# Sum and difference of the token transform made in the filter's last step; the feature transform's product order and its neighbours rearranged

## The chip, the cores and the metric

One of the cores of a Trainium2 chip runs the whole program. The metric is the device time in microseconds (us), as the median of several executions. Matrix products run on PE (TensorE; its weight loads are shown as PEld), element-wise work on DVE (VectorE), ACT (ScalarE) and POOL (GpSimd). SP issues most of the transfers, ACT and POOL a few. Every engine takes its instructions in program order and waits for the others through semaphores.

## The reference

The input x has 2048 tokens of 576 features, in fp32. Four residual layers follow each other, A, B, A, B. A is a layer norm, a sliding-window attention with 32 heads and an output projection. B is a layer norm and a global filter: a 2D real Fourier transform over tokens and features, a product with complex weights, and the transform back. Cut to that:

```python
def _B_ref(x, w_r, w_i):
    X = jnp.fft.rfft2(x, axes=(-2, -1))
    X = X * (w_r + 1j * w_i)
    return jnp.fft.irfft2(X, (S, D), axes=(-2, -1))
x = x + _A_ref(_layernorm(x), A_wqkv, A_wo)
x = x + _B_ref(_layernorm(x), B_w_r, B_w_i)
x = x + _A_ref(_layernorm(x), A_wqkv, A_wo)
x = x + _B_ref(_layernorm(x), B_w_r, B_w_i)
```

## The kernel before, in words

The change lies in `layer_b`, which runs twice. All transforms are products with constant matrices on PE. Where full precision matters, a factor is split into a high part (rounded to 12 bits, type fp32r, by ACT) and a low part (the rest, by DVE), and the product is made as high x high, high x low and low x high.

The 2048 tokens are 16 tiles of 128, token = 16 p + n2 for tile n2. Three stages follow each other.

*Filter stage* (the feature transform and the first half of the token transform), tile by tile, with the attention layer's last projection (`out.unit`, tile `ops`) running ahead in the same loop. For a tile `f0` normalises (`xn`, ACT L198; the mean and deviation come from `out.sums` on DVE and a square root on ACT L622) and folds even and odd features (`eo`, POOL L200, L202). `f1` transposes (PE L214 to L216, tile `tp`) and splits (`et`: ACT L219 high, DVE L220 low, ACT L221 a tail of 33 features). `f2` makes the feature transform `pf` (PE L231, L232: seven products for each of two halves) and splits it (`yh` ACT L235, `yl` DVE L236). `f3` makes the first half of the token transform `pz` (PE L243, six products), takes `half` out of PSUM (ACT L246), makes the sum and difference of the two halves on DVE (L247, L248) and stores them to `yd` in DRAM. In a loop for t = 1 to 11, `f1`, `f2` and `f3` of tiles t, t and t - 1 stand between the steps of later tiles; the last tiles (12 to 15) have a loop of their own, the tail. The PSUM tile `tp` has one buffer, and the turn of the attention output (`out.ahead`, tile `tpo`) uses it too.

*Mixing stage* (the filter itself), in 16 groups of frequencies. `g1m` makes a product over 16 tokens (`p`, PE L325), multiplies it by the complex weights (DVE L331 to L333) and adds the parts to `uv` (POOL L335, L336). Two groups later `g2` transforms back (`pq`, PE L347), copies the result out (`ye`, ACT L350) and stores it to `yd[1]` (L362; from ACT's queue for groups 0 to 8 and the even ones after, from SP's for the rest). The order within a turn is `g2`, `g1m`, loads.

*Inverse stage*, again in 16 tiles. `ly` loads a tile; two turns later `i0` makes the sum and difference of its two halves (POOL L382, L383, tile `both`) and splits them (ACT L384, DVE L385, and small tails L386, L387) into one of three buffers `z`, a part of `oroom`. Two turns on `i1` makes the second half of the token transform `pi` (PE L398, 18 products) and splits it (`zh` ACT L404, L406, `zl` DVE L405, L407). One turn on `i2` makes the inverse feature transform `po` (PE L418, L422, 16 products), copies one half (`bs`, ACT L425), adds the residual (DVE L426, L427) and finishes the output tile `xo` (POOL L428, L429). Program order in a turn is `ly`, `i1`, `i2`, `i0`:

```python
pipe(NT, [(0, ly), (4, i1), (5, i2), (2, i0)], lambda t: t in OPEN and nxt and next(nxt))
```

In the first of the two passes the last argument puts the opening of the next attention layer (loads, and the statistics of its first tiles) into the later turns.

Of the kernel before, what the change touches and what calls it, by code (L numbers as in the profile page):

```python
# [8 lines left out]
F32 = mybir.dt.float32  # L9
# [7 lines left out]
DF = 289  # L17
NF = 290
# [106 lines left out]
def layer_b(tc, src, dst, dcs, gc, ident, rh, rl, out, ic_d, fc_d, ga_d, m2_d, w_d, dram, nxt, share):  # L125
# [3 lines left out]
    V, A, T, P = nc.vector, nc.scalar, nc.tensor, nc.gpsimd  # L129
# [4 lines left out]
    with ExitStack() as stack:  # L134
        banks, inner = ExitStack(), ExitStack()
        ip = stack.enter_context(tc.tile_pool(name="bi", bufs=1))
        cp = inner.enter_context(tc.tile_pool(name="bc", bufs=1))
        wp = inner.enter_context(tc.tile_pool(name="bw", bufs=2))
        pp = banks.enter_context(tc.tile_pool(name="bps", bufs=2, space=PSUM))
# [42 lines left out]
        def pre(n2):  # L182

            if n2 in (1, 4, 7, 10):
                k = (1, 4, 7, 10).index(n2)
                e = 4 * k + 4 + k // 3
                nc.sync.dma_start(fc[:, 4 * k:e].rearrange("p g j c m -> p (g j c m)"), fc_d[:, 1024 * k:256 * e])
            if n2 in (2, 6, 9, 12):
                k = (2, 6, 9, 12).index(n2)
                e = 4 * k + 4 + k // 3  # L190
                nc.sync.dma_start(m2[:, 4 * k:e].rearrange("p g c m -> p (g c m)"), m2_d[:, 1024 * k:256 * e])
            if n2 % 2 and n2 // 2 < NW:
                pre_w(n2 // 2)

        def f0(n2, h):
            x, r, n = out.stats(n2)
            xn = ip.tile([128, D], F32, tag="ta", name=f"xn{n2}", bufs=3)
            A.activation(xn, x, AF.Identity, bias=n, scale=r)  # L198
            eo = h["eo"] = eos[n2 % 4]
            P.tensor_add(eo[:, 0, 1:288], xn[:, 1:288], xn[:, 575:288:-1])  # L200
            A.copy(eo[:, 0, 0:289:288], xn[:, 0:289:288])
            (P if n2 else V).tensor_sub(eo[:, 1, 0:287], xn[:, 1:288], xn[:, 575:288:-1])  # L202

            tl = h["tl"] = ip.tile([128, 2, 3, 33], F32, tag="td", name=f"tl{n2}", bufs=4)
            e = eo[:, :, 256:289]
            P.tensor_copy(tl[:, :, 0].bitcast(F32R), e)
            P.tensor_copy(tl[:, :, 2].bitcast(F32R), e)
            P.tensor_sub(tl[:, :, 1].bitcast(F32R), e, tl[:, :, 0])
# [14 lines left out]
        def f2(n2, h):  # L223
            ps = pp.tile([128, 2, 512], F32, tag="mm", name=f"pf{n2}", bufs=3)
            et = h["et"]
            for c in range(2):
                o = ps[:, c, 0:NF]
                b = 5 * c
                seq = [(0, 0), (0, 2), (2, 0), (1, 1), (1, 3), (3, 1)]
                for q, (si, mi) in enumerate(seq):  # L230
                    T.matmul(o, et[:, c, si], dcs[(b + mi) // 2][:, (b + mi) % 2], start=q == 0, stop=False)  # L231
                T.matmul(o, et[0:99, c, 4], dcs[(b + 4) // 2][0:99, (b + 4) % 2], start=False, stop=True)  # L232
            h["yh"] = yh = ip.tile([128, 2, NF], F32R, tag="yh", name=f"yh{n2}", bufs=3)
            h["yl"] = yl = ip.tile([128, 2, NF], F32R, tag="yl", name=f"yl{n2}", bufs=3)
            A.copy(yh, ps[:, :, 0:NF])  # L235
            V.tensor_sub(yl, ps[:, :, 0:NF], yh.bitcast(F32))  # L236

        def f3(n2, h):
            pz = pp.tile([128, 2, 512], F32, tag="mm", name=f"pz{n2}", bufs=3)
            yh, yl = h["yh"], h["yl"]  # L240
            for j in (1, 0):
                for k, (t, y) in enumerate(((0, yh), (0, yl), (1, yh))):
                    T.matmul(pz[:, j, 0:NF], gc[:, t, j], y[:, j], start=k == 0, stop=k == 2)  # L243
            ye = wp.tile([128, 2, NF], F32, tag="ye", name=f"ye{n2}", bufs=3)
            half = ip.tile([128, 2, NF], F32, tag="both", name=f"half{n2}", bufs=2)[:, 0]
            A.copy(half, pz[:, 1, 0:NF])  # L246
            V.tensor_add(ye[:, 0], pz[:, 0, 0:NF], half)  # L247
            V.tensor_sub(ye[:, 1], pz[:, 0, 0:NF], half)  # L248
            yef = ye.rearrange("p j f -> p (j f)")
            pre(n2)  # L250
            if n2 == FD:
                nc.sync.dma_start(y_tile(0)[0:8 * FD].rearrange("p a c f -> p a (c f)"), yd[0][0:2, 0:FD].rearrange("a n i f -> (n i) a f"))
            if n2 >= FD:
                for g in range(2):
                    (nc.scalar if n2 == NT - 1 else nc.sync).dma_start(ys[g][8 * n2:8 * n2 + 8].rearrange("p c f -> p (c f)"), yef[8 * g:8 * g + 8])
            nc.sync.dma_start(yd[0][:, n2], yef)
# [8 lines left out]
        hs = [dict() for _ in range(NT)]  # L265
# [19 lines left out]
        for t in range(1, NT - 4):  # L285
            u = t + 4
            out.unit(u, pp)
            f1(t, hs[t])
            if t == 1:
                norm(4)  # L290
                f3(0, hs[0])
                out.ahead(6, pp)
            out.sums(u)
            if t > 1:
                f3(t - 1, hs[t - 1])
            f0(u, hs[u])
            f2(t, hs[t])
            out.ahead(u + 2, pp)
        f1(NT - 4, hs[NT - 4])
# [3 lines left out]
        nc.sync.dma_start(ic.rearrange("p a f -> p (a f)").bitcast(F32), ic_d.rearrange("p a f -> p (a f)").bitcast(F32))  # L303
        nc.sync.dma_start(ga.rearrange("p a j c -> p (a j c)").bitcast(F32), ga_d.bitcast(F32))
        for t in range(NT - 4, NT + 1):
            for v, f in ((t, f2), (t + 1, f1), (t - 1, f3)):
                if v < NT:
                    f(v, hs[v])
        warm(24)
# [10 lines left out]
        def g1m(g, h):  # L320
            ps = pp.tile([128, 2, 512], F32, tag="mm", name=f"p2_{g}", bufs=3)

            for c in range(2):
                for j in range(2):
                    T.matmul(ps[64 * j:64 * j + 64, c, 0:NF], fc[:, g, j, c], h["y"][:, j], start=True, stop=g > 0)  # L325
                    if g == 0:
                        T.matmul(ps[64 * j:64 * j + 64, c, 0:NF], fc[:, 16, j, c], h["y"][:, 1 - j], start=False, stop=True)
            w = wt[g]
            p1 = tws[g % 2]
            p2 = wp.tile([128, 2, NF], F32, tag="tc", name=f"p2_{g}", bufs=3)  # L330
            V.tensor_mul(p1, ps[:, :, 0:NF], w)  # L331
            V.tensor_mul(p2[:, 0], ps[:, 0, 0:NF], w[:, 1])
            V.tensor_mul(p2[:, 1], ps[:, 1, 0:NF], w[:, 0])  # L333
            h["uv"] = uv = ip.tile([128, 2, NF], F32, tag="ta", name=f"uv{g}", bufs=3)
            P.tensor_sub(uv[:, 0], p1[:, 0], p1[:, 1])  # L335
            P.tensor_add(uv[:, 1], p2[:, 0], p2[:, 1])  # L336
# [3 lines left out]
        def g2(g, h):  # L340
            pq = pp.tile([128, 2, 512], F32, tag="mm", name=f"pq{g}", bufs=3)
            uv = h["uv"]

            for c in range(2):
                for j in range(2):
                    r = slice(64 * j, 64 * j + 64) if g else slice(0, 128)
                    T.matmul(pq[:, j, 0:NF], m2[r, g if g or j == 0 else 16, c], uv[r, c], start=c == 0, stop=c == 1)  # L347

            ye = wp.tile([128, 2, NF], F32, tag="ye", name=f"ze{g}", bufs=3) if g % 2 else eos[g // 2 % 4]
            A.copy(ye, pq[:, :, 0:NF])  # L350
            yef = ye.rearrange("p c f -> p (c f)")
            if g == FD:
                for n2 in range(2):
                    y = ys["i", n2] = yis[n2]
                    nc.sync.dma_start(y[0:8 * FD].rearrange("p c f -> p (c f)"), yd[1][n2, 0:FD].rearrange("g i f -> (g i) f"))
            if g >= FD:
                for n2 in range(2):
                    (P if n2 and g > FD else nc.sync).dma_start(ys["i", n2][8 * g:8 * g + 8].rearrange("p c f -> p (c f)"), yef.rearrange("(i n) f -> n i f", n=16)[n2])
            hold.append((g, yef))
            if g < FD or g == 15:  # L360
                for g, yef in hold:
                    (nc.sync if g % 2 and g > 8 else nc.scalar).dma_start(yd[1][:, g].rearrange("n i f -> i n f"), yef)  # L362
                hold.clear()
# [13 lines left out]
        def i0(n2, h):  # L377
            z = zs[n2 % 3]
            zf = z.bitcast(F32)
            y = h["y"]  # L380
            w = ip.tile([128, 2, NF], F32, tag="both", name=f"both{n2}", bufs=2)
            P.tensor_add(w[:, 0, 0:DF], y[:, 0, 0:DF], y[:, 1, 0:DF])  # L382
            P.tensor_sub(w[:, 1, 0:DF], y[:, 0, 0:DF], y[:, 1, 0:DF])  # L383
            A.copy(z[:, 0, :, 0:DF], w[:, :, 0:DF])  # L384
            V.tensor_sub(z[:, 1, :, 0:DF], w[:, :, 0:DF], zf[:, 0, :, 0:DF])  # L385
            A.copy(z[:, 0, :, 320:353], zf[:, 0, :, 256:289])  # L386
            V.tensor_copy(z[:, 1, :, 320:353], zf[:, 1, :, 256:289])  # L387

# [840 lines left out]
```

## Time and profile before

| | |
|---|---|
| median of 3 executions | 1576.47 us (1574.39 to 1579.74) |
| the profiled execution | 1574.53 us, span 1572.4 us |
| mean granted clock of PE | 0.963 |
| PE busy | 1464.7 us, 93% of the span |
| DVE busy | 927.3 us, 59% |
| ACT busy | 823.9 us, 52% |
| POOL busy | 715.2 us, 45% |
| DMA, over the span | 170 GB/s |

The span in 40 slices of 39 us shows where PE is not full; in the second row is the granted clock, in tenths:

```profile
PE   7999999999998898988899999999999989989887
PEclk9999999999999999978799999999999999999787
```

The slices with a low clock, 18 to 20 and 38 to 40, are the inverse stages of the two passes (from about 673 us and 1452 us); the filter and mixing stages lie ahead of them, from 489 us and 1270 us. Busy shares are averages over stages that have different limits, so the question for each edit is what its own stage waits for. The ends of matrix products in these rows are modelled; their starts are more exact.

### The profile page before, as it was taken

Reading aid. Unit: us, or ns where it says so; the run is one execution under the profiler, and the core shown is the slowest. Engines: PE = TensorE matmul, PEld = TensorE weight load, DVE = VectorE, ACT = ScalarE, POOL = GpSimd, SP = SyncE. Lnnn points to the kernel's source line nnn. Section 1 sums busy time; section 2 is a strip of 40 time slices with the busy share of each in tenths; the row PEclk is TensorE's granted clock in tenths of the full one; section 3 lists DMA queues with packets and bytes.
Section 4 is the critical chain, followed back from the end, with each engine's and each line's share of the span. In section 5 each row is a group of like instructions: output and inputs, shape, how many; then the busy total and the mean of one; then the engine's idle time right before and its main releaser. Section 6 shows DMA issues by size and latency. Waiting matters only on the chain. (4 is left out here: it accounts for less than half of the span.)

```text
span 1572.4 us, 34592 instructions
## 1 busy us (share of the span) xinstructions
PE 1464.7 (93%) x11948; PEld 1108.7 (71%) x11948; DVE 927.3 (59%) x3122; ACT 823.9 (52%) x1994; POOL 715.2 (45%) x1188
## 2 busy tenths in 40 slices
PE   7999999999998898988899999999999989989887
PEld 7976666666558887577799756666665578965776
DVE  4338777777844554534452487777778455544443
ACT  5525777777783443222354166777777744432322
POOL 2186455555572331533322954455545633315333
PEclk9999999999999999978799999999999999999787
DMA  6657456565543556656253675555555536576431
GB/s 204 177 183 230 149 180 195 170 185 170 175 122 120 185 181 220 234 168 217 98 164 89 199 223 172 157 157 156 162 151 152 151 107 207 180 238 212 159 121 61
DMA packets 203240, 266.59 MB, mean 170 GB/s; under 512 B 103938, under 2 KB 109058, under 8 KB 202234
## 3 DMA queue, kind: packets, MB, share of 16 engines
q1 hardware_dynamic: 192890, 242.23, 50.1%
q10 hardware_dynamic: 7808, 15.62, 3.0%
q0 software_dynamic: 2368, 6.53, 1.6%
q8 instruction: 96, 1.57, 0.4%
q14 instruction: 78, 0.64, 0.1%
HBM read 165.66 MB, written 101.47 MB: 170 GB/s over the span
## 5 line engine op out<-in xcount | busy, mean ns | idle before, releaser
L893 DVE CUSTOM_DVE_ANT_0 jk<-S,mask 128x384 bf16<-128x384 f32 (+2 forms) x1024 | 490.6, 529 | 110.6 <-PE E L928 57.1
L929 ACT ACTIVATE P<-E 128x384 f32<-128x384 f32 (+2 forms) x1024 | 409.1, 476 | 123.3 <-PE E L928 99.7
L931 POOL TENSOR_SCALAR_AFFINE_SELECT P<-P 128x512 f32<-128x512 f32 x256 | 163.1, 637 | 276.6 <-ACT P L929 253.7
L891 PE MATMUL S<-ks,qs 63*128 63x384 f32 (+2 forms) x1024 | 268.9, 371 | 0.6 <-DVE m L893 0.4
L928 PE MATMUL E<-qs,ks 64*128 64x384 f32 (+2 forms) x1024 | 222.3, 372 | 4.7 <-ACT P L929 2.1
L891 PEld LDWEIGHTS S<-ks,qs 63*128 63x128 f32 x1024 | 140.4, 184 | 104.7 <-DVE m L893 72.8
L948 PE MATMUL U<-P,vq 128*19 128x128 f32 (+1 forms) x3840 | 187.8, 328 | 1.0 <-ACT us L953 1.0
L834 PE MATMUL pj<-xh,wqh 128*128 128x512 f32 x360 | 156.0, 433 | 2.9 <-ACT vt L778 1.7
L948 PEld LDWEIGHTS U<-P,vq 128*19 128x19 f32 x3840 | 95.8, 98 | 77.6 <-issue 21.5
L934 POOL TENSOR_SCALAR_AFFINE_SELECT P<-P 128x512 f32<-128x512 f32 x224 | 142.6, 637 | 0.0
L928 PEld LDWEIGHTS E<-qs,ks 64*128 64x128 f32 x1024 | 114.1, 185 | 19.4 <-ACT P L929 7.7
L591 PE MATMUL ops<-oroom 128*128 128x288 f32 x840 | 122.3, 301 | 4.4 <-DVE oroom L574 3.0
L834 PE MATMUL pj<-xh,wql 128*128 128x512 f32 x360 | 124.5, 419 | 0.4 <-POOL wql L496 0.4
L834 PE MATMUL pj<-xl,wqh 128*128 128x512 f32 x288 | 121.6, 422 | 0.0
L591 PEld LDWEIGHTS ops<-oroom 128*128 128x128 f32 x840 | 114.4, 191 | 6.2 <-DVE oroom L574 4.0
L398 PE MATMUL pi<-oroom 128*128 128x128 f32 (+1 forms) x576 | 89.5, 316 | 29.4 <-ACT oroom L384 21.7
L398 PEld LDWEIGHTS pi<-oroom 128*128 128x128 f32 (+1 forms) x576 | 83.2, 230 | 37.4 <-ACT oroom L384 26.1
L200 POOL TENSOR_TENSOR eo<-xn 128x287 f32<-128x287 f32 x32 | 26.1, 816 | 164.2 <-ACT xn L198 148.4
L834 PEld LDWEIGHTS pj<-xh,wqh 128*128 128x128 f32 x360 | 67.6, 188 | 34.3 <-issue 10.6
L385 DVE TENSOR_TENSOR oroom<-both,oroom 128x578 fp32r<-128x578 f32 x32 | 25.2, 788 | 109.0 <-ACT oroom L384 109.0
L893 DVE DVE_READ_ACCUMULATOR2_ANT m<- 128x1 f32 x1024 | 85.4, 83 | 0.0
L428 POOL TENSOR_TENSOR xo<-xo,bs 128x289 f32<-128x289 f32 x32 | 25.8, 807 | 130.2 <-DVE xo L426 126.3
(185 smaller groups left out, 2727.0 us busy)
## 6 DMA issues: line engine op xcount, KB each, us to landing
qk_d<-sg SPq DMA_DIRECT2D x56, 512.0 KB
qs<-qk_d SPq DMA_DIRECT2D x384, 72.0 KB
ks<-qk_d SPq DMA_DIRECT2D x348, 72.0 KB
v_d<-vt SPq DMA_DIRECT2D x32, 304.0 KB
vq<-v_d SPq DMA_DIRECT2D x16, 608.0 KB
yd<-ye SPq DMA_DIRECT2D x32, 290.0 KB
wt<-in_w SPq DMA_DIRECT2D x16, 580.0 KB
x<-ofree SPq DMA_DIRECT2D x32, 288.0 KB
```

The costliest lines, as they stand in the source:

```text
L200: P.tensor_add(eo[:, 0, 1:288], xn[:, 1:288], xn[:, 575:288:-1])
L398: T.matmul(o, z[:, sl, c, lo:lo + m], mo, start=k == 0, stop=k == 2)
L428: P.tensor_add(xo[:, 0:DF], xo[:, 0:DF], bs[:, 0:DF])
L591: self.nc.tensor.matmul(self.ps[u][n][:, 0:288], x, self.w[p][:, wk * D + n * 288:wk * D + n * 288 + 288], start=first and i == 0, stop=la ...
L834: T.matmul(box["ps"].rearrange("r (n p) -> r n p", n=NT) if second else box["ps"], w[:, wk], x, start=s == 0, stop=s == len(ks) - 1)
L891: T.matmul(ps[:, 0:N], q[b:b + 63, pair, i * 128:i * 128 + 128], k[b:b + 63, pair, lo:hi], start=True, stop=True)
L893: V.tensor_tensor_reduce(out=jk[:, 0:N], in0=ps[:, 0:N], in1=mask[:, 384 - N:384], scale=1.0, scalar=-3e38, op0=ALU.add, op1=ALU.max, accu ...
L928: T.matmul(ps[:, 0:nq], k[b:b + 64, pair, j * 128:j * 128 + 128], q[b:b + 64, pair, j * 128:j * 128 + nq], start=True, stop=True)
L929: A.activation(p[:, hl_, 0:nq], ps[:, 0:nq], AF.Exp, scale=SC)
L931: P.affine_select(out=p[:, :, 0:128], in_=p[:, :, 0:128], pattern=[[0, 4], [1, 128]], compare_op=ALU.is_ge, fill=0.0, base=0, channel_mult ...
L934: P.affine_select(out=p[:, :, 256:384], in_=p[:, :, 256:384], pattern=[[0, 4], [-1, 128]], compare_op=ALU.is_gt, fill=0.0, base=0, channel ...
L948: T.matmul(U[32 * h:32 * h + 19, (q0 % 4) * 128:(q0 % 4) * 128 + 128 * (q1 - q0)], vts[n][:, j, h], pt[n, j][:, h, (q0 - j) * 128:(q1 - j) ...
```

## The change

Four things, all in `layer_b`:

- The sum and difference of the two halves move from the inverse stage's `i0` (POOL, both) into the mixing stage's `g2`: ACT copies `pq` into `both`, DVE makes the sum, POOL the difference, and these are stored. `i0` splits the loaded tile as it is.
- In `g1m` two products of DVE become one of twice the width, with the order of the weights' halves reversed.
- `f2` issues the four products that need only the high part of `et`, for both halves, ahead of the three that need the low part and the tail.
- `f3` keeps only its products; taking `pz` out, the DVE sums and the stores become `f4`, which stands behind `f0` in the loop. `f3` stands ahead of the statistics. In the tail, `f1` of the next tile goes ahead of `f2`.

```diff
 def f2(n2, h):
...
-    for c in range(2):
-        o = ps[:, c, 0:NF]
-        b = 5 * c
-        seq = [(0, 0), (0, 2), (2, 0), (1, 1), (1, 3), (3, 1)]
-        for q, (si, mi) in enumerate(seq):
-            T.matmul(o, et[:, c, si], dcs[(b + mi) // 2][:, (b + mi) % 2], start=q == 0, stop=False)
-        T.matmul(o, et[0:99, c, 4], dcs[(b + 4) // 2][0:99, (b + 4) % 2], start=False, stop=True)
+    for seq in ([(0, 0), (0, 2), (1, 1), (1, 3)], [(2, 0), (3, 1), (4, 4)]):
+        for c in range(2):
+            for si, mi in seq:
+                b = 5 * c + mi
+                r = slice(0, 99 if si == 4 else 128)
+                T.matmul(ps[:, c, 0:NF], et[r, c, si], dcs[b // 2][r, b % 2], start=mi == si == 0, stop=si == 4)
...
+def f4(n2, h):
+    pz = h["pz"]
     ye = wp.tile([128, 2, NF], F32, tag="ye", name=f"ye{n2}", bufs=3)
...
             if t == 1:
                 norm(4)
                 f3(0, hs[0])
                 out.ahead(6, pp)
+            else:
+                f3(t - 1, hs[t - 1])
             out.sums(u)
-            if t > 1:
-                f3(t - 1, hs[t - 1])
             f0(u, hs[u])
+            f4(t - 1, hs[t - 1])
             f2(t, hs[t])
...
-            for v, f in ((t, f2), (t + 1, f1), (t - 1, f3)):
+            for v, f in ((t + 1, f1), (t, f2), (t - 1, f3), (t - 1, f4)):
...
-            V.tensor_mul(p2[:, 0], ps[:, 0, 0:NF], w[:, 1])
-            V.tensor_mul(p2[:, 1], ps[:, 1, 0:NF], w[:, 0])
+            V.tensor_mul(p2, ps[:, :, 0:NF], w[:, ::-1])
...
-            A.copy(ye, pq[:, :, 0:NF])
+            both = ip.tile([128, 2, NF], F32, tag="both", name=f"both{g}", bufs=2)
+            A.copy(both, pq[:, :, 0:NF])
+            V.tensor_add(ye[:, 0], both[:, 0], both[:, 1])
+            P.tensor_sub(ye[:, 1], both[:, 0], both[:, 1])
...
 def i0(n2, h):
-    y = h["y"]
-    w = ip.tile([128, 2, NF], F32, tag="both", name=f"both{n2}", bufs=2)
-    P.tensor_add(w[:, 0, 0:DF], y[:, 0, 0:DF], y[:, 1, 0:DF])
-    P.tensor_sub(w[:, 1, 0:DF], y[:, 0, 0:DF], y[:, 1, 0:DF])
-    A.copy(z[:, 0, :, 0:DF], w[:, :, 0:DF])
-    V.tensor_sub(z[:, 1, :, 0:DF], w[:, :, 0:DF], zf[:, 0, :, 0:DF])
+    A.copy(z[:, 0, :, 0:DF], h["y"][:, :, 0:DF])
+    V.tensor_sub(z[:, 1, :, 0:DF], h["y"][:, :, 0:DF], zf[:, 0, :, 0:DF])
```

How instructions stand on an engine, first POOL in the inverse stage before; `xo` is an output tile, `both` the sum and difference of a later one, `ofree` the memory that holds the loaded tiles:

```order
L382 TENSOR_TENSOR both_10215<-ofree 128x289
L383 TENSOR_TENSOR both_10215<-ofree 128x289
L428 TENSOR_TENSOR xo_10265<-xo_10265,bs_10266 128x289
L429 TENSOR_TENSOR xo_10265<-xo_10265,bs_10266 128x287
L382 TENSOR_TENSOR both_10273<-ofree 128x289
L383 TENSOR_TENSOR both_10273<-ofree 128x289
```

and with the change, three output tiles in a row (L429 and L430 are the former L428 and L429):

```order
L429 TENSOR_TENSOR xo_10416<-xo_10416,bs_10417 128x289
L430 TENSOR_TENSOR xo_10416<-xo_10416,bs_10417 128x287
L429 TENSOR_TENSOR xo_10475<-xo_10475,bs_10476 128x289
L430 TENSOR_TENSOR xo_10475<-xo_10475,bs_10476 128x287
L429 TENSOR_TENSOR xo_10530<-xo_10530,bs_10531 128x289
L430 TENSOR_TENSOR xo_10530<-xo_10530,bs_10531 128x287
```

POOL has nothing left between two output tiles there, and nothing on ACT or DVE waits for POOL to make `both`.

Second, POOL in the mixing stage before, three groups:

```order
L335 TENSOR_TENSOR uv_9876<-ofree 128x290
L336 TENSOR_TENSOR uv_9876<-p_10_9872 128x290
L335 TENSOR_TENSOR uv_9896<-ofree 128x290
L336 TENSOR_TENSOR uv_9896<-p_11_9892 128x290
L335 TENSOR_TENSOR uv_9915<-ofree 128x290
L336 TENSOR_TENSOR uv_9915<-p_12_9911 128x290
```

and with the change (L337 and L338 are the former L335 and L336; `ze` and `eo` are the buffers that are stored):

```order
L355 TENSOR_TENSOR eo_8106<-both_9879 128x290
L337 TENSOR_TENSOR uv_9892<-ofree 128x290
L338 TENSOR_TENSOR uv_9892<-p_10_9889 128x290
L355 TENSOR_TENSOR ze_9900<-both_9901 128x290
L337 TENSOR_TENSOR uv_9914<-ofree 128x290
L338 TENSOR_TENSOR uv_9914<-p_11_9911 128x290
```

The difference of a finished group stands ahead of the two sums of the group that is two later. On DVE the sum (L354) stands in the same way ahead of that group's products, and on ACT the issue of the store stands between two copies.

Third, ACT in one loop of the filter stage before:

```order
L219 CAST et_8772<-tp_8765 128x2x256
L221 CAST et_8772<-tp_8765 99x2x128
L622 ACTIVATE ofree<-ofree,eps 128x1
L246 COPY half_8788<-pz_8780 128x290
L198 ACTIVATE xn_8796<-ofree 128x576
L201 COPY eo_8108<-xn_8796 128x2
L235 CAST yh_8820<-pf_8805 128x580
```

and with the change (L623, L248 and L234 are the former L622, L246 and L235):

```order
L219 CAST et_8772<-tp_8765 128x2x256
L221 CAST et_8772<-tp_8765 99x2x128
L623 ACTIVATE ofree<-ofree,eps 128x1
L198 ACTIVATE xn_8789<-ofree 128x576
L201 COPY eo_8108<-xn_8789 128x2
L248 COPY half_8799<-pz_8776 128x290
L234 CAST yh_8820<-pf_8805 128x580
```

The copy of `half`, and with it the two sums on DVE and the stores on SP, now stand behind the normalisation of the later tile.

More of the change, by code (lines that the diff above doesn't have):

```diff
@@ L238, in f3 @@
         def f3(n2, h):
-            pz = pp.tile([128, 2, 512], F32, tag="mm", name=f"pz{n2}", bufs=3)
+            pz = h["pz"] = pp.tile([128, 2, 512], F32, tag="mm", name=f"pz{n2}", bufs=3)
             yh, yl = h["yh"], h["yl"]
```

## The prediction

> **What bounds the kernel now.** I read the mean busy time by stretches first, then the chain of waits inside the last stage, then the rows of that stage, engine by engine, in order of time. First the stretches: time, busy time (and instructions) of PE, PEld, DVE, ACT and POOL, then PE's clock, DMA share, GB/s. The stretches are the filter loop, the mixing stage and the inverse token stage of the second pass.
>
> ```profile
> 1290.00:1380.00 90.00, 82.91 (x594) 76.91 (x592) 51.65 (x137) 40.61 (x94) 29.28 (x71) 1.00 0.60 189
> 1404.00:1445.00 41.00, 39.31 (x265) 20.76 (x266) 23.84 (x48) 9.73 (x16) 22.93 (x33) 1.00 0.66 231
> 1470.00:1556.00 86.00, 70.77 (x405) 66.57 (x406) 34.77 (x72) 24.75 (x61) 33.12 (x48) 0.77 0.33 110
> ```
>
> In the filter loop PE is busy 92% and in the mixing stage 96%, both at full clock. In the inverse stage nothing is full: PE 82% at a clock of 0.77, every other engine under 41%, DMA a third. Such a stage is held by a ring of waits. The chain of waits, cut to that stretch, in order of time (start, length, what), comes back to the same place after each token tile:
>
> ```profile
> 1474.56 0.69 POOL xo L429
> 1475.25 0.65 POOL both L382
> 1475.90 0.66 POOL both L383
> 1476.58 0.69 ACT oroom L384
> 1477.29 0.77 DVE oroom L385
> ...
> 1481.74 0.69 POOL xo L429
> ...
> 1553.65 0.69 POOL xo L429
> ```
>
> From 1474.56 to 1553.65 lie 11 turns of 7.19 us. POOL ends one output tile (L428, L429), only then makes the sum and difference of a later tile (L382, L383); ACT copies it (L384), DVE splits it (L385), and because ACT and DVE work in order, the next tile's feature split follows and leads to the next output tile on POOL. The timeline of ACT, DVE and POOL over the rest of the turn (start, duration, engine, line):
>
> ```profile
> 1478.24 0.58 ACT L404 CAST zh<-pi 128x512 fp32r<-128x512 f32 x1
> 1479.85 0.41 ACT L425 COPY bs<-po 128x290 f32<-128x290 f32 x1
> 1480.44 0.46 DVE L426 TENSOR_TENSOR xo<-ofree,po 128x289 f32<-128x289 f32 x1
> 1480.82 0.45 DVE L427 TENSOR_TENSOR xo<-ofree,po 128x287 f32<-128x287 f32 x1
> 1480.98 0.81 POOL L428 TENSOR_TENSOR xo<-xo,bs 128x289 f32<-128x289 f32 x1 [4.43 <-DVE xo L426]
> 1481.74 0.69 POOL L429 TENSOR_TENSOR xo<-xo,bs 128x287 f32<-128x287 f32 x1
> ```
>
> **The inverse stage: POOL leaves the ring.** L382 and L383 are gone; ACT's copy and DVE's split read the loaded tile itself. What is late next? Count from the feature copy L404 (1478.24). L425 starts at +1.61, L427 at +2.58. ACT's copy (0.69) now stands right behind L425: +2.02 to +2.71. DVE's split stands behind L427, at about +2.98. In the trace the next L404 follows the split's start by 1478.24 - 1477.29 = 0.95. So ACT and DVE alone turn in 3.93 us. PE needs, by its timeline:
>
> ```profile
> 1465.42 1.97 PE L398 MATMUL pi<-oroom 128*128 128x128 f32 x18
> 1467.22 0.48 PE L418 MATMUL po<-oroom,zh 128*128 128x290 f32 x2
> ...
> 1469.15 0.43 PE L422 MATMUL po<-oroom,zh 97*128 97x290 f32 x2
> ```
>
> 18 products in 1.80, and 16 in 1.93 + 2 x 0.14 = 2.21: 4.01 us a tile at full clock. One cost is new. The split has two inputs in SBUF, and POOL's L428 (+2.74 to +3.55) now runs when it wants to start; before, POOL was idle then. The trace has such overlaps: DVE and POOL at two places, and the usual length of the small DVE operation (min/median/max).
>
> ```profile
> 786.22 0.80 POOL L428 TENSOR_TENSOR xo<-xo,bs 128x289 f32<-128x289 f32 x1 [1.57 <-issue]
> 786.56 0.49 DVE L734 SCALAR_TENSOR_TENSOR nb<-mv,rs 128x1 f32<-128x1 f32 x1
> 786.99 0.69 POOL L429 TENSOR_TENSOR xo<-xo,bs 128x287 f32<-128x287 f32 x1
> L734 DVE SCALAR_TENSOR_TENSOR nb<-mv,rs x32: 159/159/516, 5.2 to 839.5; 128x1 f32<-128x1 f32 x32
> 1453.64 0.69 POOL L383 TENSOR_TENSOR both<-ofree 128x289 f32<-128x289 f32 x1
> 1453.76 1.19 DVE L385 TENSOR_TENSOR oroom<-both,oroom 128x578 fp32r<-128x578 f32 x1 [10.48 <-ACT oroom L384]
> ```
>
> L734 ends at 787.05, just as POOL's L428 does (787.02), although L429 follows at once: DVE waits for the running POOL operation and gets in between two. L385 ends 0.62 after L383 does (1454.95 against 1454.33). So the split ends at 3.55 + 0.62 = +4.17, 0.43 later than without, and the next L404 comes 1478.24 - 1478.05 = 0.19 after the split's end: a turn of 4.36. That exceeds PE's 4.01, so it is my value; the bounds are 4.01 (no collision) and 5.0 (POOL's L429 goes first as well: +0.65). The Trainium skill, page "SBUF — State Buffer", section "Who interferes with whom", says that a VectorE instruction with two SBUF inputs and a GpSimd instruction that reads SBUF exclude each other for the whole instruction; by it the turn is 4.36 or more, without it 4.01, and the two places above agree with it.
>
> Twelve turns x (7.19 - 4.36) = 34.0 us a pass, and the two POOL operations ahead of the stage's first ACT copy go too, 1.3: 35.3. In the first pass the next block's opening shares the stage; its statistics on DVE stand in the new ring:
>
> ```profile
> L726 DVE BATCH_NORM_STATS2 st<-ax 128x6 f32<-128x288 f32 x64 | 26.0, 448 | 3.0 <-DMA ax<-in_x 2.9
> ```
>
> Two of 0.45 in five of the turns: 4.5 at most, 0 if hidden; I take 3. Together -35.3 - 32.3 = -67.6, bounds -52 (turn 5.0) and -76 (turn 4.01). The loads keep up: 0.33 of the DMA engines at 7.19 a turn is 0.54 at 4.36, and SP's loads, no longer ahead of a POOL read, still have two turns before their use.
>
> **The filter stage.** PE and ACT in one loop of the first pass, and its last rows at the tail's entry:
>
> ```profile
> 555.02 0.53 PE L231 MATMUL pf<-dc,et 128*128 128x290 f32 x2
> 555.75 0.81 PE L231 MATMUL pf<-dc,et 128*128 128x290 f32 x4 [0.19 <-DVE et L220]
> 556.90 0.38 ACT L246 COPY half<-pz 128x290 f32<-128x290 f32 x1
> 558.49 0.87 ACT L198 ACTIVATE xn<-ofree 128x576 f32<-128x576 f32 x1 [1.21 <-issue]
> 562.07 0.33 PE L214 MATMUL tp<-ident,eo 128*128 128x128 f32 x1 [0.17 <-DVE oroom L586]
> 563.62 0.54 PE L231 MATMUL pf<-dc,et 128*128 128x290 f32 x2
> ...
> 602.74 0.53 PE L231 MATMUL pf<-dc,et 128*128 128x290 f32 x2 [2.38 <-ACT et L219]
> ```
>
> A loop is 8.60 us. The first two products leave at 0.14 each (as po above), so the third waits 0.73 - 0.28 = 0.45 for DVE's low part; with eight high-part products first (1.1 us) it doesn't. The second stall (0.17) ends with a chain through xn; xn now goes ahead of the half copy and of two DVE sums, about 1.0 earlier, of which the copy takes back 0.4. So 0 to 0.62 a loop; I take 0.5, near the sum of the two stalls: ten loops, two passes, -10. At the tail f1 of the next tile is put ahead of f2 on PE: later turns lose the same 0.45 stall, but the first f2 now waits also for the second transposes, which wait for the first tile's copies. The 2.38 idle may grow by 1 to 2 and PE come out of it at half clock. Three stalls off against that: 0, bounds -3 and +3 a pass.
>
> **The mixing stage pays.** A group now needs one DVE sum and one POOL difference more, between ACT's copy and the store. PE, POOL, ACT and ACT's queue in a group:
>
> ```profile
> 1436.98 1.25 PE L347 MATMUL pq<-uv,m 64*128 64x290 f32 x8
> 1439.29 1.25 PE L347 MATMUL pq<-uv,m 64*128 64x290 f32 x8
> 1438.75 0.70 POOL L336 TENSOR_TENSOR uv<-p 128x290 f32<-128x290 f32 x1
> 1438.28 0.64 ACT L350 COPY eo<-pq 128x580 f32<-128x580 f32 x1 [1.66 <-PE pq L347]
> 1438.95 0.58 ACTq L362 DMA_DIRECT2D yd<-eo  x1
> ```
>
> A group takes PE 2.31. POOL goes from two to three operations of 0.70, with gaps 2.2: just below. DVE's new sum reads SBUF twice and starts with POOL's difference, from the same copy; the holds lift POOL to about 2.5. Over some ten groups +0.2, +2 a pass, and at the stage's end one POOL operation (0.7) stands ahead of the last store: +5.4 in all. If nothing collides, only the ends: +1.4. Upper bound: ACT's yd issue now waits for POOL's difference, and behind it stands ACT's next copy; the ring copy 0.64, sum 0.45, product to uv 0.84, uv 0.70 twice, difference 0.70, issue 0.58 is 4.6, 5.5 with hops and two collisions, and spans two groups: 2.75, +0.44 x 28 = +12. One merged DVE product saves 0.1 a group off the path: nothing.
>
> **The sum**, against the profiled execution (1574.5; the three runs' median 1576.5 is 0.1% above it, less than the 0.3% that a measurement here can tell): -67.6 - 10 + 5.4 = -72.2, 1502.
>
> **The rivals.** (B) POOL keeps its turn and the split waits for L429 too: 5.0 a turn, 24 x 0.64 = 15 slower, 1517. L734's row speaks against it, but that is a tiny operation.
> (C) No collision matters: PE's 4.01 rules, 24 x 0.35 = 8 less, and 4 less in the mixing stage: 1490.
> (D) PE stays cold in the inverse stage. Cold rows:
>
> ```profile
> 1491.70 0.44 PE L398 MATMUL pi<-oroom 128*128 128x128 f32 x2 [1.56 <-ACT oroom L384]
> 1492.50 3.38 PE L398 MATMUL pi<-oroom 128*128 128x128 f32 x16 [0.36 <-DVE oroom L385]
> ```
>
> 16 take 3.38, so 18 take 3.8, and a tile about 7.7: the old turn, and the gain is gone: 1570; cold for half the turns, 1535. Here 1.9 us of gaps were enough to halve the clock; a closed loop at 4.36 has gaps of 0.35, and the filter loop, whose gaps are 0.6, ran at full clock. The Trainium skill, page "TensorE: Matmul & The Clock Gate", section "What's actually happening", has the clock fall after an idle window of 3.4 us; the rows show less being enough, and by either the new loop stays warm unless loads run late.
> (E) Slower: the mixing ring closes in one group instead of two. Then a group is 5.5, +3.2 x 28 = +90 in place of +5.4: 1586. It decides from +2.8 a group (78 us of gain over 28 groups). Against it: program order gives it two groups, since a group's product runs two groups before its copy.
>
> **Chances.** Forecast 0.62, B 0.12, C 0.12, D 0.09 (some of it below 1530), E 0.04, no change 0.01. The range 1484 to 1528 takes in B and C with the unknowns of the filter and mixing stages and leaves out D's worst and E. Faster 0.94, same 0.02, slower 0.04.
>
> **What would show it.** The inverse stage without L382 and L383, turns of 4.0 to 4.4 and PE's clock near 1.00; the split 1.2 long where L428 runs; no wait before the third pf product, a loop of about 8.1; mixing groups of 2.3 to 2.6. I am wrong if the turn is above 5.5, if the clock stays below 0.9 there, or if a group passes 3.

## The result, and the profile after

The changed kernel took 1489.9 us (median of 4, 1487.7 to 1499.5) beside 1578.1 us for the kernel before in the same rounds: a ratio of 0.945 [0.940, 0.950]. In a second measurement it was 1497.6 us beside 1579.4, 0.948 [0.946, 0.951]. The forecast was 1502 in 1484 to 1528: the direction was right, and so was the mechanism in the inverse stage, which gives most of the gain; the gain was a little larger.

The profiled execution took 1487.7 us (span 1486.0, before 1572.4). From the timeline's PE rows, from the first product of a stage to the first of the next, in us:

| stage | before, pass 1 | after | before, pass 2 | after | both passes | predicted |
|---|---|---|---|---|---|---|
| filter (`pf` to `p`) | 127.3 | 121.6 | 127.6 | 120.1 | -13.2 | -10 |
| mixing (`p` to the last `pq`) | 40.0 | 42.6 | 40.0 | 42.4 | +5.1 | +4.0 |
| entry (last `pq` to `pi`) | 10.3 | 8.4 | 9.3 | 8.6 | -2.6 | -1.2 |
| inverse (`pi` to the last `po`) | 111.2 | 74.8 | 110.1 | 71.9 | -74.6 | -65.0 |
| the rest | | | | | -1.0 | 0 |
| span | | | | | -86.4 | -72.2 |

(The 1.3 a pass that the prediction counted at the inverse stage's head, and the 0.7 at the mixing stage's end, stand in the row of the entry.) In the profile of the second measurement the four rows are -13.7, +5.0, -0.8 and -71.3. So a few us of these differences belong to the run.

The busy time by stretches, for the changed kernel: filter loop, mixing stage and inverse stage of the second pass (columns as before).

```profile
1255.00:1320.00 65.00, 64.15 (x475) 61.40 (x476) 40.51 (x107) 31.36 (x72) 22.60 (x56) 1.00 0.66 217
1356.00:1396.00 40.00, 38.31 (x252) 18.34 (x249) 29.55 (x47) 9.63 (x15) 33.52 (x46) 1.00 0.68 233
1422.00:1472.00 50.00, 48.72 (x402) 47.81 (x401) 42.06 (x69) 22.59 (x57) 23.42 (x24) 1.00 0.53 178
```

The inverse stage went from PE busy 82% at a clock of 0.77 to 97% at 1.00. In the mixing stage POOL is now at 84% (before 56%). The chain of waits of the changed kernel in the inverse stage:

```profile
1443.73 1.15 DVE oroom L386
1444.91 0.25 ACT oroom L387
1445.16 0.50 ACT zh L405
1445.68 0.70 DVE zl L406
...
1447.72 0.36 DVE xo L428
1448.09 1.15 DVE oroom L386
```

POOL is gone from it: the ring runs through ACT and DVE, and a turn is 1448.09 - 1443.73 = 4.36 us. The next rows, from the timeline, show the split (L386) between POOL's two operations:

```profile
1443.45 0.81 POOL L429 TENSOR_TENSOR xo<-xo,bs 128x289 f32<-128x289 f32 x1 [2.37 <-DVE xo L427]
1443.65 1.23 DVE L386 TENSOR_TENSOR oroom<-ofree,oroom 128x578 fp32r<-128x578 f32 x1
1444.21 1.22 POOL L430 TENSOR_TENSOR xo<-xo,bs 128x287 f32<-128x287 f32 x1
1444.91 0.57 DVE L388 CAST oroom<-oroom 128x66 fp32r<-128x66 f32 x1
```

The split ends 0.62 after L429 does (1444.88 against 1444.26). L430, which stood next on POOL, takes 1.22, and the small copy L388 ends with L430 (1445.48 and 1445.43).

### The profile page after: what moved, and what is told of

Its sections match the earlier page's. It is cut to its first block, busy times and chain, and to the rows that moved or that the text cites. A ratio compares the mean times of both kernels' runs of the same rounds, so it can differ in the third digit from the quotient of the medians.

```text
span 1486.0 us, 34682 instructions
## 1 busy us (share of the span) xinstructions
PE 1412.5 (95%) x11948; PEld 1065.5 (72%) x11948; DVE 959.0 (65%) x3122; ACT 821.8 (55%) x1994; POOL 712.9 (48%) x1156
## 4 chain that ended last, share of the span: by engine, by line
PE 57%; DVE 13%; ACT 9%; DMA 6%; POOL 4%; issue 3%; SPq 1%; ACTq 1%; DVEq 0%; POOLq 0%
PE pj L835 16%; PE S L892 11%; PE U L949 10%; PE E L929 4%; PE vps L775 4%; PE ops L592 3%; DVE oroom L386 2%; PE tpo L963 2%; PE pf L231 2%; DMA ofree<-yd 2%; ACT P L930 2%; ACT xn L198 1%; DVE ofree L621 1%; DVE zl L406 1%; DVE yl L235 1%
## 5 line engine op out<-in xcount | busy, mean ns | idle before, releaser
L835 PEld LDWEIGHTS pj<-xh,wqh 128*128 128x128 f32 x360 | 67.6, 188 | 34.5 <-issue 10.6
L850 DVE TENSOR_TENSOR sg<-pj,sg 128x512 fp32r<-128x512 f32 x72 | 49.5, 687 | 58.6 <-ACT sg L847 58.6
L835 PEld LDWEIGHTS pj<-xh,wql 128*128 128x128 f32 x360 | 64.2, 189 | 21.0 <-issue 10.7
L847 ACT CAST sg<-pj 128x512 fp32r<-128x512 f32 x72 | 42.2, 586 | 61.4 <-PE pj L835 46.4
L429 POOL TENSOR_TENSOR xo<-xo,bs 128x289 f32<-128x289 f32 x32 | 25.9, 808 | 101.0 <-DVE xo L427 101.0
```

What stands on the lines that cost most here:

```text
L835: T.matmul(box["ps"].rearrange("r (n p) -> r n p", n=NT) if second else box["ps"], w[:, wk], x, start=s == 0, stop=s == len(ks) - 1)
L847: A.copy(rest[:, 0], by)
L850: V.tensor_sub(rest[:, 1], by, rest[:, 0].bitcast(F32))
```

## The experiments

The theory: the old turn of 7.19 us was a ring of waits that went through POOL's order of work, and PE's low clock followed from it; the new turn of 4.36 is a ring through ACT and DVE that holds one collision with POOL. The rivals: PE's half clock held the turn; the amount of POOL's work did; the collision is hidden behind PE. Two more questions came with the result, on the mixing stage and on the filter loop.

**One part at a time.** The move alone (`e1_move`: the edits of `g2` and `i0` on the kernel before), and the filter stage's edits alone (`e2_filter`: `f2`, `f3`/`f4`, the order in the loop and in the tail; it keeps the merged DVE product of `g1m` as well, and its groups in the mixing stage take 2.31 as before).

> The kernel before with one part of the change: sum and difference are made after the mixing copy (g2), and the inverse stage (i0) reads the loaded tile. The filter stage stays as before. Theory (each part of the change works in its own stage): inverse stages and what leads into them shorter by about 77 us for two passes, mixing stages longer by 5, filter stages within 1 us of before: about -72 us, a ratio of 0.954. Rival (the parts feed each other, for example through PE's clock at a stage's start): the filter stages move too, or the sum of this run's and the next run's differences misses -86 us by more than 5.

> The kernel before with the filter stage's edits alone: high-part products first, the next tile's normalization ahead of the half copy and its two sums, and the new order at the stage's tail. Theory: filter loops of 8.07 us in place of 8.60, filter stages 6 and 7 us shorter, nothing elsewhere: -13 us, a ratio of 0.992. Rival: less than 5 us, and the rest of what the filter stage gained in the whole change came from the other part.

The move alone: 1506.6 us, 0.955 [0.953, 0.956]; inverse stages 75.5 and 73.4, mixing 43.3 and 43.0, filter 126.3 and 127.6. The filter edits alone: 1566.8 us, 0.9925 [0.991, 0.994], filter stages 120.3 and 120.0. The product of the two ratios is 0.947, inside what the whole change gave. So the parts work each in its own stage, as far as the profiles can tell. The mixing stage costs 0.6 a pass more in the first run than in the whole change: its groups take 2.50 there and 2.43 with the merged DVE product, which the prediction had put at nothing.

**Is it the ring?** The kernel before, with all its POOL operations, but `i0` written between `i1` and `i2`:

```diff
-pipe(NT, [(0, ly), (4, i1), (5, i2), (2, i0)], ...)
+pipe(NT, [(0, ly), (4, i1), (2, i0), (5, i2)], ...)
```

> The kernel before, with sum and difference still on POOL in the inverse stage, but the step that makes them (i0) written between the feature step (i1) and the output step (i2) instead of behind both: POOL then makes them ahead of the output tile's two operations in each turn, ACT copies and DVE splits them ahead of their output operations. Theory (a ring through POOL's order of work sets the old 7.19 us): the ring becomes ACT copy 0.7, split 0.8, ACT's small copy 0.25, output copy 0.4, POOL output 0.8 and 0.7, sum 0.65, difference 0.7: about 5.0 us a turn, so some 2.1 x 25 = -53 us with every POOL operation still there, a ratio of 0.966. Rival 1 (what counts is how much POOL and the shared tile buffers carry): 7.2, no change. Rival 2 (PE's half clock sets the turn): above 6.5 us.

1530.1 us, 0.971 [0.968, 0.974]; the inverse stages fell to 90.4 and 84.6 us. The chain of waits of this run:

```profile
1483.27 0.70 POOL xo L429
1483.96 0.65 POOL both L382
1484.61 0.66 POOL both L383
1485.29 0.69 ACT oroom L384
...
1487.04 0.31 ACT bs L425
...
1487.38 0.47 DVE xo L426
...
1488.67 0.69 POOL xo L429
```

A turn is 5.40 us, with the same POOL operations in the same lengths. So what POOL carries did not set 7.19; where its work stands in the order of ACT and DVE did. I expected 5.0: the ring is the one I named, but I left out DVE's L426, which stands between ACT's L425 and POOL's output operations and takes about 0.5. Order alone gives -46 us in the inverse stages, the move alone -72.

**Is it the clock?** The kernel before with 18 idle products behind each output tile:

```diff
+wm = pp.tile([128, 2, 512], F32, tag="tp", name=f"wm{n2}", bufs=1)
+for k in range(18):
+    T.matmul(wm[:, 0, 0:NF], ic[:, 0, 0:128], ic[:, 0], start=True, stop=True)
```

> The kernel before, with 18 idle products of 128x290 behind each output tile of the inverse stage: PE then has 4.0 + 2.5 = 6.5 us of work in a turn at full clock, and the clock should stay near 1.0. Theory (the ring of waits through POOL sets the turn, the low clock only follows from it): the turn stays at 7.2 us, the whole time within 10 us of before. Rival (the half clock held the turn up, and the change gains by warming PE): with a full clock the turn falls below 6.8.

1581.4 us beside 1574.3. A stretch of its inverse stage, and its chain of waits:

```profile
1490.00:1530.00 40.00, 38.36 (x306) 37.91 (x305) 16.41 (x34) 11.49 (x28) 15.31 (x23) 1.00 0.37 122
```

```profile
1522.05 0.69 POOL xo L429
1522.74 0.65 POOL both L382
1523.39 0.67 POOL both L383
...
1529.24 0.69 POOL xo L429
```

The clock is 1.00, and the turn is still 1529.24 - 1522.05 = 7.19. So the low clock did not hold the turn; it came with PE's gaps (0.77 at turns of 7.19, 0.91 at the 5.40 of `e3_order_before`, 1.00 at 4.36).

**The collision.** Two runs take it out of the inverse stage. `e5_nofinish` is the changed kernel without the two POOL operations (L429, L430), so that the part of the output that `bs` brings is missing. `e4_order_after` is the changed kernel with `i0` between `i1` and `i2` (the diff above), so that the split runs before the output operations of its turn, while POOL is idle.

> The changed kernel without POOL's two operations on the output tile (the part of the output that the second sum brings is left out). The order on the other engines stays as it is. Theory (DVE's split waits for POOL): the split takes 0.76, the turn falls from 4.36 to 4.0 to 4.1 us. Rival (ACT and DVE alone, or PE, make 4.36): the turn stays at 4.3 or more.

> The changed kernel, with i0 written between i1 and i2: DVE's split then runs while POOL has nothing to do. Theory (DVE's wait for POOL's running operation sets the turn of 4.36): the split takes 0.76 and not 1.23, its small copy 0.20 and not 0.57, POOL's second output operation 0.69 and not 1.22, and the turn falls to PE's 4.0 to 4.1 us: 0.3 x 26 = -8 us against the changed kernel, a ratio of 0.939 to the kernel before. Rival (the turn is PE's own 4.2 with its hops, the collision is hidden): 4.3 to 4.4, no difference to the changed kernel.

Groups of instructions in the second inverse stage (1420 to 1470 us): first the order experiment, then the split of the run without POOL's operations.

```profile
L386 DVE TENSOR_TENSOR oroom<-ofree,oroom 128x578 fp32r<-128x578 f32 x12 | 9.1, 760 | 1.8 <-ACT oroom L385 0.5
L430 POOL TENSOR_TENSOR xo<-xo,bs 128x287 f32<-128x287 f32 x12 | 8.3, 692 | 0.0
L388 DVE CAST oroom<-oroom 128x66 fp32r<-128x66 f32 x12 | 2.4, 196 | 0.4
```

```profile
L386 DVE TENSOR_TENSOR oroom<-ofree,oroom 128x578 fp32r<-128x578 f32 x10 | 7.5, 754 | 0.0
```

Without POOL's operations the one execution took 1474.4 us. The split takes 0.76 and 0.75, and PE starts a new `pi` every 4.00 us in both; the second inverse stage takes 67.7 us in both, 4.1 less than in the changed kernel. So the collision cost 0.36 a turn, and behind it stands PE's own 4.0. The rule that I quoted from the Trainium skill (page "SBUF — State Buffer", section "Who interferes with whom") holds here: 1.23 with POOL's reads beside the split, 0.76 without. The whole time of `e4_order_after` did not follow: 1488.4 us, 0.9435 [0.940, 0.947], where I expected 0.939, and not clear of the changed kernel. Its first inverse stage took 76.5 us. A turn there was 7.32, and the timeline shows what for:

```profile
721.90 0.67 ACT L385 CAST oroom<-ofree 128x578 fp32r<-128x578 f32 x1 [2.64 <-DMA ofree<-yd]
```

The copy stands earlier in the turn, and its load came 2.6 us too late. SP had issued that load (L380) at 712.05, behind two loads of weights for the next block's opening (L716). It landed at 721.88, 9.8 us later; the same loads of the second pass landed after 3.2 to 5.8 us. The DMA share was 0.91 from 710 to 715 us, and full from 715 to 722. The second pass has no opening and no such wait, so the opening's loads are the likely cause; no run took them out.

**The mixing stage.** The chain of waits of the changed kernel goes round there once in two groups. The timeline's rows of one such turn, on ACT's queue, ACT, DVE and POOL:

```profile
1373.10 0.58 ACTq L367 DMA_DIRECT2D yd<-eo  x1
1373.77 0.64 ACT L353 COPY both<-pq 128x580 f32<-128x580 f32 x1 [1.79 <-DVE ofree L334]
1374.44 0.50 DVE L354 TENSOR_TENSOR ze<-both 128x290 f32<-128x290 f32 x1 [0.60 <-ACT both L353]
1374.86 0.75 DVE L334 TENSOR_TENSOR ofree<-p,wt 128x580 f32<-128x580 f32 x1
1375.69 0.70 POOL L337 TENSOR_TENSOR uv<-ofree 128x290 f32<-128x290 f32 x1 [0.20 <-DVE ofree L334]
1376.36 0.70 POOL L338 TENSOR_TENSOR uv<-p 128x290 f32<-128x290 f32 x1
1377.01 0.91 POOL L355 TENSOR_TENSOR eo<-both 128x290 f32<-128x290 f32 x1
1377.96 0.57 ACTq L367 DMA_DIRECT2D yd<-eo  x1
```

The store's issue waits for POOL's difference, and ACT's next copy stands behind the issue. DVE's sum needs the copy, the product to `uv` (L334) stands behind the sum, POOL's two sums to `uv` need the products, and the difference of the next group stands behind these two, and with it its store. That takes 1377.96 - 1373.10 = 4.86 for two groups, 2.43 for each, above PE's 2.31. The difference takes 0.91 where POOL's other operations of that size take 0.70. In `e7_psadd` the sum on DVE reads one operand in PSUM:

```diff
-V.tensor_add(ye[:, 0], both[:, 0], both[:, 1])
+V.tensor_add(ye[:, 0], pq[:, 0, 0:NF], both[:, 1])
```

> The changed kernel, with DVE's sum in the mixing stage reading one operand in PSUM (the first half of the product) and only the other from ACT's copy, so that it has one input in SBUF and not two. Theory (DVE and POOL collide on operations that read SBUF twice; that is the 0.12 us that a group grew): the sum no longer waits for POOL, the group falls from 2.43 towards 2.31 us and the mixing stages by 1 to 2 us each. Rival (the third POOL operation alone fills POOL, or ACT's queue waits): groups stay at 2.4 or more.

```profile
1375.67 0.46 DVE L354 TENSOR_TENSOR ze<-pq,both 128x290 f32<-128x290 f32 x1 [0.46 <-ACT both L353]
1375.94 0.70 POOL L355 TENSOR_TENSOR ze<-both 128x290 f32<-128x290 f32 x1
1376.67 0.58 ACTq L367 DMA_DIRECT2D yd<-ze  x1
1377.35 0.64 ACT L353 COPY both<-pq 128x580 f32<-128x580 f32 x1 [1.72 <-PE pq L349]
```

The difference takes 0.70, ACT's copy waits for PE, and groups are back at 2.31; the mixing stages take 40.4 and 40.2. Three POOL operations in a group fit; it was the collision that made the ring longer than PE's work. The one execution as a whole took 1489.0, no less than the changed kernel's 1487.7: its entries and inverse stages were 5.5 longer in sum. Two executions of the changed kernel differ by about as much: the same rows are 5.1 longer in its second profile than in its first.

**The filter loop.** It went from 8.60 to 8.07 us. `e8_f2only` is the kernel before with the product order alone; `e10_oldf2` is the kernel before with the other edits of the filter stage, and the merged product, but the old product order.

> The kernel before with the product order of the filter stage alone (high parts of both halves first). Theory: of the 0.53 us a loop that the filter stage gained, 0.45 is the wait before the third product: a loop of about 8.15 to 8.2 us, and the second stall (0.17, through the normalization) stays. Rival: the other chain takes over, and the loop stays above 8.4 until the normalization is moved as well.

> The kernel before with the next tile's normalization ahead of the half copy and its sums, and the new tail order, but the old product order in the filter stage. Two theories for the loop that fell from 8.60 to 8.07 when all edits were made and stayed at 8.59 with the product order alone. Theory 1 (the chain through normalization, transposes and high part closes the loop; the wait before the third product lies off it): the loop falls to 8.1 here too. Theory 2 (each edit opens only one of two chains of nearly the same length): the loop stays at 8.4 or more, since the wait before the third product closes it then.

One execution each took 1574.5 and 1571.5 us. The timeline's rows of a loop, first with the product order alone, then with the filter stage's other edits, then in the changed kernel:

```profile
1325.47 2.16 PE L231 MATMUL pf<-dc,et 128*128 128x290 f32 x14
1328.94 0.87 ACT L198 ACTIVATE xn<-ofree 128x576 f32<-128x576 f32 x1 [1.21 <-issue]
1332.51 0.33 PE L214 MATMUL tp<-ident,eo 128*128 128x128 f32 x1 [0.61 <-DVE oroom L585]
```

```profile
1322.94 0.81 PE L231 MATMUL pf<-dc,et 128*128 128x290 f32 x4 [0.20 <-DVE et L220]
1324.66 0.87 ACT L198 ACTIVATE xn<-ofree 128x576 f32<-128x576 f32 x1 [0.48 <-DVE ofree L630]
```

```profile
1280.87 2.17 PE L231 MATMUL pf<-dc,et 128*128 128x290 f32 x14
1283.32 0.87 ACT L198 ACTIVATE xn<-ofree 128x576 f32<-128x576 f32 x1 [0.47 <-DVE ofree L628]
```

With the product order alone the 14 products run without a wait, and the loop is 8.59: PE now waits 0.61 at the transposes instead, for a split on DVE (L585), and the normalization still starts 3.47 after the first product. With the normalization moved and the old products the loop is 8.22, with both 8.07. So neither theory as I put it: the chain through the normalization closed the loop, and moving it gave 0.38; only then does the wait before the third product count, for 0.15 more. In the changed kernel the chain of waits runs through the normalization again: from the transposes to the statistics, L198, the copy of `half`, the two sums and the later splits on ACT and DVE, back to the transposes in 8.07.

**A version without the collisions.** The changed kernel with the sum out of PSUM, `i0` ahead of `i2` in the turn, and all steps behind the load one turn later:

```diff
-OPEN = *range(7, 20, 2), 20
+OPEN = *range(8, 21, 2), 21
...
-V.tensor_add(ye[:, 0], both[:, 0], both[:, 1])
+V.tensor_add(ye[:, 0], pq[:, 0, 0:NF], both[:, 1])
...
-pipe(NT, [(0, ly), (4, i1), (5, i2), (2, i0)], ...)
+pipe(NT, [(0, ly), (5, i1), (3, i0), (6, i2)], ...)
```

> The changed kernel without its two collisions of DVE and POOL: the mixing sum reads one operand in PSUM, and in the inverse stage the split stands before the output operations in each turn, by a pipeline that is one step deeper after the load (load 0, i0 3, i1 5, i2 6; the next block's opening one step later too). The deeper pipeline gives a load one turn more before its use, since in the run with i0 between i1 and i2 one turn of the first pass waited 2.6 us for a load. Theory: mixing groups 2.31, inverse turns 4.0 in both passes: mixing 2 x 2.2, the second inverse stage 4, the first 3 to 7 shorter than in the changed kernel, about 1475 us by the profile, a ratio of 0.936 to the kernel before. Rival (what one stage gains the next loses at the loads or the opening): a ratio of 0.940 or more.

1481.3 us, 0.937 [0.935, 0.940]; mixing stages 40.2 and 40.2, inverse stages 69.7 and 68.3. Inverse stretches of the first and the second pass:

```profile
690.00:735.00 45.00, 44.03 (x371) 43.65 (x371) 33.47 (x76) 21.41 (x56) 17.57 (x25) 1.00 0.77 269
1420.00:1465.00 45.00, 45.00 (x386) 45.00 (x386) 32.22 (x69) 22.61 (x56) 16.74 (x23) 1.00 0.57 186
```

PE is busy 98% and 100%. The changed kernel and this version once more, measured side by side:

> The changed kernel itself, measured in the same rounds as the version without collisions, since the intervals of the two (0.940 to 0.950 and 0.935 to 0.940) touch. If that version's gain of 8 us is real: 0.941 to 0.945 here.

> The version without collisions once more, beside the changed kernel. If its gain is real: 0.936 to 0.939, at least 0.004 below the changed kernel. If it was noise of the rounds: the two within 0.002.

The changed kernel 1497.6 us, 0.948 [0.946, 0.951], a little above what I expected; the version without collisions 1482.2 us, 0.938 [0.936, 0.940]. It beats both kernels, and is 0.0105 below the changed one.

## Why the prediction was right, point by point

**The ring and its successor** were read rightly: with L382 and L383 gone the turn is 4.36, by the hops and the collision that the sum was made of; the clock is 1.00 and the split 1.2 long. The term was too small, 65.0 without the head against 74.6 (71.3 in the second profile). Three sizes were off. Twelve turns were put at 7.19 - 4.36 = 2.83 each, -34.0; in the second pass they gave -35.8, because the first four ran at PE's 4.0 before the ring took over. (The second profile has no such turns in that pass: there the twelve gave -34.5.) The first three turns and the last tile gave another -2.4 there and -1.2 in the first pass, which I had not counted. And the opening of the next block in the first pass cost 1.3 (two turns of 5.0), not 3; the twelve turns of that pass gave -35.1 with it.

The loads kept up. In the second pass the DMA share is 0.53, where I took 0.54. In the first pass I had not counted the loads of the opening. With them the share is 0.97 between 700 and 725 us of the changed kernel, and that is where the other order of `e4_order_after` met its late load.

**The filter term** (-10, measured -13.2) had the loop's size right, 0.53 where I took 0.5, and its reason wrong, so that the size is luck. The step that failed is "the third waits 0.45; with eight high-part products first it doesn't", taken as a gain by itself: the wait goes, the gain does not come, as the loop was closed elsewhere. The tails gave 1 and 3 a pass, where I took 0 with a bound of 3.

**The mixing term** (+4.0 in the stage without its ends, measured +5.1) had about the right size and the wrong carrier, which is luck too. I let POOL fill up to 2.5 a group. What closed was the ring that I gave as the upper bound: issue, copy, sum, product to `uv`, the two sums to `uv`, difference, over two groups. It is 4.86 long and not 5.5, so that a group takes 2.43 and not 2.75; the one collision that the rows show in it, on POOL's difference, costs 0.91 - 0.70 = 0.21.

**The rivals.** B (POOL keeps its turn, 5.0) did not come: DVE gets in before L430, and POOL pays. C (4.01 a turn) is what the kernel does without the collision, at the price that I gave, 0.35. D fell with the clock of 1.00, and the idle products showed that a warm PE would not have changed the old turn. E and "no change" are out by the result.

## What to carry to other kernels

The stage where no engine was full was held by a ring of waits. In such a place, follow the chain until it returns to the same instruction, and see whether another place in the program order opens it before work is moved. A wait that vanishes is a gain only if the chain of waits went through it; in the filter loop a wait of 0.45 us could be removed for nothing. Two engines that held each other up could be parted here without less work: in time, by order, or by taking one operand from PSUM; but an operation that moves ahead needs its load earlier, and the order paid in both passes only with a deeper pipeline.

## What the hardware showed that I had not expected

The collision was paid by both sides. DVE's split took 1.23 in place of 0.76, and POOL's next operation 1.22 in place of 0.69, although it was ready and its predecessor had just ended. A small DVE copy with one input in SBUF (128x66) took 0.57 beside POOL and 0.20 alone. The Trainium skill, page "SBUF — State Buffer", section "Who interferes with whom", has the engine that issues first keep the shared ports for the whole instruction, and says that copies can enter modes in which they contend. The rows agree with the first; which mode the copy ran in they don't show. I had weighed only the split.
